# A fused attention and feed-forward kernel: beta turned early, longer fp32 dummies in the head, one tile written in halves, a zero fill moved behind a cast

## The chip, the cores and the metric

The kernel runs on one core of a Trainium2 chip. PE is TensorE (PEld its weight loads), DVE is VectorE, ACT is ScalarE, POOL is GpSimd. The metric is the device time in microseconds (us), the median over several executions. The profile times one execution's "span" on the core; it is about 1.8 us shorter than the device time. All timed executions below are in the fast state; one single run (e5) is of state unknown, as single runs on one core are. Ratios are the mean time of one kernel's fast runs over that of the other's fast runs of the same rounds, so they are not quite the ratio of the medians quoted.

## The reference

```python
# q, k, v: (8, 8, 576, 64) f32;  w_in: (512, 2048);  w_out: (2048, 512);  beta: (2048,)
q_s = softmax(q, over the 64 features);   k_s = softmax(k, over the 576 positions)
kv  = einsum('bhsd,bhse->bhde', k_s, v)
x   = einsum('bhsd,bhde->bhse', q_s, kv)  -> 4608 tokens x 512
h   = x @ w_in
out = (h * sigmoid(beta * h)) @ w_out     # float32
```

## The kernel before

The tokens are worked off in nine slabs of 512. A slab has "pass 1" (16 tiles f of 4 matmuls m with `WIN`, then a Silu on ACT) and "pass 2" (64 matmuls with `WOUT`). Everything before the first pass 1 is the head: it loads Q, K and V of batch 0 and the weights, takes exponentials (`EQ`, `EK`), transposes the queries on PE, forms the small KV matrices (`KVD`) and the tile `XT`.

`w_in` comes in five column chunks. They are loaded as fp32 and cast to bf16 by POOL (chunk 0, half of 1) and DVE (the rest). Chunk 1 serves tiles 2 and 3, chunk 2 tiles 4 to 7, chunk 3 tiles 8 to 11, chunk 4 tiles 12 to 15.

```python
WCH = ((0, 256), (256, 256), (512, 512), (1024, 512), (1536, 512))   # first column, width
...
def homes_ek(i, e_, r=()):                       # zeros in EK, on POOL
    z = EK[i][64 * e_:64 * e_ + 64, :, :, 64 * (1 - e_):64 * (2 - e_)]
    add(POOL, lambda e: e.memset(z.bitcast(F32), 0.0), r=r, w=[("ekz", i, e_)])
...
def warm(n, bk, long=False):                     # dummies that keep PE busy
    w = WARM[:, :].bitcast(F32) if long else WARM
    for _ in range(n):
        mm(PS[bk][:, 0:256] if long else PS[bk][:, :], w[:, 0:128], w[:, :], True, True, ...)
...                                              # the head, in program order
warm(6, 0, True)
exp_q(0); exp_kh(...)                            # ACT
norm_main(0, 0, 1); norm_main(0, 1, 1, POOL)     # softmax of the queries
go(t_steps(0, (0,), HEAD))                       # 4 transposes on PE
warm(3, 0, True)
norm_main(0, 2, 1, POOL); norm_main(0, 3, 1)
go(t_steps(0, (1,), HEAD))
warm(1, 0, True)
for m in (0, 2): load_win(0, m, 2)
for c in range(1, len(WCH)): load_win(c)
cast_v(...)
for m in range(NM): cast_win(0, m, 1, POOL)
cast_win(1, 0, 2, POOL)
for e_ in range(2):
    homes_ek(1, e_, [("win", 3, NM - 1)])        # nothing has written ("win", 3, 3) yet: no wait
go(t_steps(0, (2,), HEAD))
turn_beta()                                      # 6 tiny fp32 transposes
cast_v(0, 1, DVE)
go(t_steps(0, (3,), (1,)))
ksum(...); warm(2, 0)
...
out_now(0, 0, 4, ACTE)                           # XT of head pair 0, copied whole by ACT
...
cast_win(1, 2, 2, DVE)                           # second half of chunk 1
for m in range(1, NM): at(m)                     # tiles 0 and 1
for c in range(2, len(WCH)):
    for m in range(NM): cast_win(c, m, 1, DVE)
```

Dependencies are found in program order: an operation waits for the last writer of a key that stands before it. So the read of `("win", 3, 3)` in `homes_ek` did nothing. During pass 2 of slab 0, the attention of batch 1 is done at fixed steps (one step per matmul); `TT` and the `out_now(1, ...)` calls belong to that. I call it the crossing.

The softmax here doesn't subtract the row's maximum and nothing guards it: scores larger than these inputs give would overflow.

## Time and profile before

| | before |
|---|---|
| timed runs | 287.0 us median (286.8 to 287.31) |
| the execution that was profiled | 287.53 us, span 285.7, mean granted clock 0.992 |
| PE busy | 97% of the span |

The page's second part shows the span in 40 slices of 7.1 us, digits in tenths.

```profile
PE   7999999999999999999999999999999999999994
...
PEclk9899999999999999999999999999999999999999
DMA  7999999995899999207970033002800020021022
```

PE is full after the first slice, so only the head and the places where PE waits have time to give. The clock is below full in the second slice, and DMA is at 90% or more from the second to the ninth. The windows view of before shows the first of these closer. Its columns are the window, its length, busy us of PE, PEld, DVE, ACT and POOL with their instruction counts, the granted clock, the DMA share and GB/s.

```profile
10.00:12.00 2.00, 2.00 (x32) 1.58 (x32) 1.62 (x5) 1.98 (x2) 0.88 (x2) 0.88 1.01 377
12.00:14.00 2.00, 1.79 (x29) 1.56 (x28) 0.73 (x4) 0.50 (x2) 1.54 (x4) 0.50 1.03 349
14.00:16.00 2.00, 1.95 (x16) 0.94 (x15) 0.75 (x3) 1.17 (x2) 1.41 (x4) 0.76 1.07 381
```

The clock records of the trace put it exactly: 0.5 from 11.53 to 14.95 us. The first record is at 4.71 us, and the views print 1.00 before it; but the dummies there come 0.427 us apart, and 0.216 after it, so PE began at half clock. "Clock 1.00" below means from the first record on. The waits of PE (who waited for whom, us in total, times, longest):

```profile
PE PS L364 <- DVE WARM L221: 1.2, 1, 1.2
PE PS L362 <- DVE EQ L332: 0.6, 1, 0.6
PE PS L364 <- DVE WIN L585: 0.6, 1, 0.6
PE PS L364 <- DVE KVD L401: 0.5, 2, 0.3
PE PS L362 <- POOL EQ L332: 0.4, 2, 0.2
```

The timeline of DVE in before (start, us, operation, count, idle before it) shows the casts of chunk 1 (first line), 2, 3 and 4:

```profile
17.25 1.36 DVE L585 CAST WIN<-WST 128x512 bf16<-128x512 f32 x1
...
18.69 1.36 DVE L585 CAST WIN<-WST 128x512 bf16<-128x512 f32 x4
22.02 1.43 DVE L585 CAST WIN<-O2S 128x512 bf16<-128x512 f32 x4 [1.97 <-DMA O2S<-in_moe_w_in_dram]
24.73 1.44 DVE L585 CAST WIN<-O2S 128x512 bf16<-128x512 f32 x4 [1.27 <-DMA O2S<-in_moe_w_in_dram]
```

The timeline of POOL in before, the zero fill:

```profile
16.17 2.16 POOL L237 MEMSET EK<- 64x1152 f32 x2
```

And of PE in before: the wait for chunk 1, and the start of pass 2.

```profile
18.67 11.83 PE L364 MATMUL PS<-XT,WIN 128*128 128x512 bf16 x54 [0.55 <-DVE WIN L585]
30.34 1.03 PE L364 MATMUL PS<-WOUT,GT 128*128 128x512 bf16 x4
```

One cast of chunk 1 took 1.36 us where four casts of the same shape took 1.36 us together, and PE waited for it. At the crossing, PE's timeline of before has the wait for KVD and the first matmuls of slab 1:

```profile
45.17 0.39 PE L364 MATMUL PS<-QT,KVD 128*128 128x512 bf16 x1 [0.28 <-DVE KVD L401]
...
46.49 0.59 PE L364 MATMUL PS<-XT,WIN 128*128 128x512 bf16 x2
```

### The profile page before, as it was taken

How to read it: one execution, taken by the hardware profiler on the slowest of the kernel's cores; microseconds unless marked ns; L12 is line 12 of the kernel's file. 1: busy time of each engine (PE TensorE's matmuls, PEld its weight loads, DVE VectorE, ACT ScalarE, POOL GpSimd, SP SyncE). 2: the span in 40 equal slices, each digit the busy share in tenths (PEclk: the TensorE clock that was granted, in tenths of full speed). 3: DMA queues.
4: the chain of work that ended last, by engine and by line, in shares of the span. 5: the costliest groups of instructions: out<-in, count | busy, mean ns of one | idle time of the engine just before them, and what ended most of it. 6: DMA issues, size and time to landing. Idle time of an engine off the chain costs nothing.

```text
span 285.7 us, 3896 instructions
## 1 busy us (share of the span) xinstructions
PE 278.5 (97%) x1586; PEld 138.5 (48%) x1586; DVE 115.8 (41%) x212; ACT 177.4 (62%) x241; POOL 38.7 (14%) x60
## 2 busy tenths in 40 slices
PE   7999999999999999999999999999999999999994
PEld 5645445444455445544454445444544444444441
DVE  3765696109691248114741564055705200110021
ACT  5788486889977945796479737892650186028500
POOL 6640031305303032300140000000000000000000
PEclk9899999999999999999999999999999999999999
DMA  7999999995899999207970033002800020021022
GB/s 244 376 384 414 384 384 379 307 389 102 228 411 218 385 330 345 59 13 239 384 119 1 2 147 75 2 1 106 131 4 0 30 119 0 0 87 62 0 73 73
DMA packets 41438, 50.07 MB, mean 175 GB/s; under 512 B 20166, under 2 KB 29386, under 8 KB 40140
## 3 DMA queue, kind: packets, MB, share of 16 engines
q1 hardware_dynamic: 40556, 48.77, 53.6%
q10 hardware_dynamic: 864, 1.05, 1.1%
q8 instruction: 12, 0.20, 0.3%
q14 instruction: 6, 0.05, 0.1%
HBM read 36.71 MB, written 9.44 MB: 161 GB/s over the span
## 4 chain that ended last, share of the span: by engine, by line
PE 94%; DVE 2%; DMA 1%; POOL 1%; issue 0%; ACT 0%; POOLq 0%
PE PS L364 93%; DMA QF<-in_q_dram 1%; PE PS L362 1%; POOL EQ L332 1%; DVE QS L330 0%; DVE WIN L585 0%; DVE KVD L401 0%; DVE XT L534 0%; DVE EQ L332 0%; DVE O2S L726 0%; ACT EQ L293 0%; DVE QI L331 0%; DVE BC L605 0%; DVE RC L422 0%; DVE BETA L608 0%
## 5 line engine op out<-in xcount | busy, mean ns | idle before, releaser
L672 ACT ACTIVATE GT<-PS,BETA 128x512 bf16<-128x512 f32 x144 | 97.5, 688 | 77.9 <-PE PS L364 77.8
L364 PE MATMUL PS<-XT,WIN 128*128 128x512 bf16 x576 | 132.2, 379 | 0.6 <-DVE WIN L585 0.6
L364 PE MATMUL PS<-WOUT,GT 128*128 128x512 bf16 x576 | 132.7, 379 | 0.0
L364 PEld LDWEIGHTS PS<-XT,WIN 128*128 128x128 bf16 x576 | 60.1, 106 | 59.6 <-DVE WIN L585 1.0
L364 PEld LDWEIGHTS PS<-WOUT,GT 128*128 128x128 bf16 x576 | 54.6, 98 | 62.8 <-DVE O2S L726 0.2
L726 DVE COPY O2S<-PS 128x512 f32<-128x512 f32 x34 | 23.3, 686 | 110.7 <-PE PS L364 110.7
L364 PE MATMUL PS<-VB,EK 128*128 128x65 bf16 (+2 forms) x306 | 36.6, 197 | 0.0
L349 POOL CAST VB<-VF 128x576 bf16<-128x576 f32 (+1 forms) x31 | 22.7, 732 | 73.0 <-DMA VF<-in_v_dram 37.4
L305 ACT ACTIVATE EK<-KF 64x1152 bf16<-64x1152 f32 x24 | 27.8, 1158 | 0.4
L364 PEld LDWEIGHTS PS<-VB,EK 128*128 128x128 bf16 x306 | 23.0, 102 | 7.2 <-issue 0.5
L330 DVE TENSOR_REDUCE QS<-EQ 128x8 f32<-128x512 bf16 (+1 forms) x22 | 20.1, 914 | 3.6 <-ACT EQ L293 3.5
L439 DVE CAST XT<-PS 128x512 bf16<-128x512 f32 x24 | 16.4, 690 | 10.9 <-PE PS L364 10.9
L293 ACT ACTIVATE EQ<-QF 128x512 bf16<-128x512 f32 x32 | 17.9, 619 | 4.6 <-DMA QF<-in_q_dram 4.3
L332 DVE TENSOR_TENSOR EQ<-EQ,QI 128x1024 bf16<-128x1024 bf16 (+1 forms) x15 | 16.4, 1093 | 0.5
L364 PE MATMUL PS<-QT,KVD 128*128 128x512 bf16 (+1 forms) x36 | 12.4, 366 | 0.5 <-DVE KVD L401 0.5
L332 POOL TENSOR_TENSOR EQ<-EQ,QI 128x512 bf16<-128x512 bf16 x7 | 7.3, 1042 | 32.9 <-DVE QI L331 32.6
L315 ACT ACTIVATE EK<-KF 64x1152 bf16<-64x1152 f32 (+1 forms) x10 | 9.5, 966 | 1.6 <-DMA KF<-in_k_dram 1.5
L364 PE MATMUL PS<-WARM 128*128 128x256 f32 (+1 forms) x22 | 7.5, 490 | 1.2 <-DVE WARM L221 1.2
L401 DVE TENSOR_TENSOR KVD<-PS,RC 64x128 bf16<-64x128 f32 (+1 forms) x22 | 7.7, 349 | 1.6 <-PE PS L364 0.9
L338 DVE TENSOR_REDUCE QRS<-EQR 128x8 f32<-128x512 bf16 x4 | 2.7, 680 | 13.4 <-ACT EQR L320 13.4
L672 ACT ACT_TABLE_LOAD x5 | 6.4, 1283 | 0.1
L293 ACT ACT_TABLE_LOAD x5 | 6.4, 1283 | 0.1
(50 smaller groups left out, 77.9 us busy)
## 6 DMA issues: line engine op xcount, KB each, us to landing
out_dram<-O2S SPq DMA_DIRECT2D x8, 1024.0 KB, 5.2
KF<-in_k_dram SPq DMA_DIRECT2D x6, 1152.0 KB, 8.3
VF<-in_v_dram SPq DMA_DIRECT2D x6, 1152.0 KB, 11.9
QF<-in_q_dram SPq DMA_DIRECT2D x6, 1024.0 KB, 7.5
KF<-in_k_dram SPq DMA_DIRECT2D x8, 288.0 KB, 7.4
VF<-in_v_dram SPq DMA_DIRECT2D x8, 288.0 KB, 7.4
O2S<-in_moe_w_in_dram SPq DMA_DIRECT2D x2, 1024.0 KB, 13.6
WST<-in_moe_w_out_dram SPq DMA_DIRECT2D x2, 1024.0 KB, 9.2
```

Source lines behind the costliest of these rows:

```text
L293: add(ACTE, lambda e, o=o, a=a: e.activation(o, a, ACT.Exp), r=[("qf", i, hp)], w=[("eq", i, hp)])
L305: add(ACTE, lambda e, o=o, a=a: e.activation(o, a, ACT.Exp), r=[("kf", i, h) for h in hps], w=[("ek", i, h, e_) for h in hps])
L315: add(ACTE, lambda e: e.activation(o, a, ACT.Exp), r=[("kf", i, h) for h in hps], w=[("ek", i, h, e_) for h in hps])
L330: add(DVE, lambda e: e.tensor_reduce(s_, a, AX.X, ALU.add), r=ks, w=[("qs", i, hp0)])
L332: add(eng, lambda e: e.tensor_tensor(a, a, vb, ALU.mult), r=ks + [("qi", i, hp0)], w=ks)
L349: add(eng, lambda e: (e.copy if eng == ACTE else e.tensor_copy)(o, a), r=[("vf", i, hp), ("vone", i)], w=[("vb", i, hp, h) for h in ((0, 1 ...
L362: add(PE, lambda e: e.transpose(o, l, r_), r=r, w=w, bank=[bk])
L364: add(PE, lambda e: e.matmul(o, l, r_, start=start, stop=stop), r=r, w=w, bank=[bk])
L401: add(DVE, lambda e, o=o, a=a, s_=s_: e.tensor_tensor(o, a, s_, ALU.mult), r=[("ps", bk)] + [("rc", i, h) for h in hps], w=[("kvd", i, h, ...
L439: add(eng, lambda e: (e.copy if eng == ACTE else e.tensor_copy)(XT[i][:, hp, :], PS[bk][:, :]), r=[("ps", bk)], w=[("xt", i, hp)], bank=[bk])
L672: add(ACTE, lambda e: e.activation(GT[:, f, :], PS[bk][:, :], ACT.Silu, scale=BETA[:, f:f + 1]), r=[("ps", bk), "beta"], w=[("gt", f)], ba ...
L726: add(eng, lambda e: (e.copy if eng == ACTE else e.tensor_copy)(O2S[t % 2][:, u, :], PS[bk][:, :]), r=[("ps", bk)], w=[("o2", t % 2, u)], ...
```

## The change

The intent is to keep PE's clock up through the head and to let pass 1 start sooner. There are five parts: (1) the dummies become fp32 matmuls of 512 columns, placed between all the transposes; (2) beta is loaded right behind the first queries and turned after the first transposes, where PE would idle; (3) `XT` of pair 0 is copied in halves by DVE and ACT; (4) the zero fill of the second `EK` is moved behind the casts, so that its gate is real; (5) at the crossing, `out_now(1, 0)` and `out_now(1, 1)` come at the last step.

```diff
+        add(DVE, lambda e: e.memset(XT8[:, 0:2, :].bitcast(F32), 0.0), w=["xw"])
...
         def warm(n, bk, long=False):
-            w = WARM[:, :].bitcast(F32) if long else WARM
             for _ in range(n):
-                mm(PS[bk][:, 0:256] if long else PS[bk][:, :], w[:, 0:128], w[:, :], True, True,
-                   r=["warm"], w=[("ps", bk)], bk=bk)
+                if long:
+                    mm(PS[bk][:, :], bass.AP(XT8, 0, [[NM * SM, 128], [1, 256]]).bitcast(F32),
+                       bass.AP(XT8, 0, [[NM * SM, 128], [1, 1024]]).bitcast(F32), True, True,
+                       r=["xw"], w=[("ps", bk)], bk=bk)
+                else: ...                                      # as before
...
-        load_k(0, 4)
         for i, n in enumerate((2, 4)): ...                     # the load of beta
+        load_k(0, 4)
...
-        warm(6, 0, True)
+        warm(3, 0, True)
...
         go(t_steps(0, (0,), HEAD))
-        warm(3, 0, True)
+        turn_beta()
+        warm(1, 0, True)
...
-        for e_ in range(2):
-            homes_ek(1, e_, [("win", 3, NM - 1)])
         go(t_steps(0, (2,), HEAD))
-        turn_beta()
+        warm(1, 0, True)
...
-            if t < 2 and m > 1:
+            if (t, m) in ((0, 0), (0, 2), (0, 3), (1, 2), (1, 3)):
...
-        TT = (116, 126.5)
+        TT = (116, 128)
...
-        out_now(0, 0, 4, ACTE)
+        out_halves(0, 0, 4, 6)
...
         for c in range(2, len(WCH)):
             for m in range(NM):
                 cast_win(c, m, 1, DVE)
+        for e_ in range(2):
+            homes_ek(1, e_, [("win", 3, NM - 1)])
...
-                todo += [(126, lambda: out_now(1, 0, 7, DVE))]
+                todo += [(127.5, lambda: (out_now(1, 0, 7, DVE), out_now(1, 1, 1, ACTE)))]
...
-                out_now(1, 1, 1, ACTE)
```

Cut: the numbers of PSUM banks, and one key that guards XT8's later use.

More of the change, by code (lines that the diff above doesn't have):

```diff
@@ L471, in one @@
                     add(DVE, lambda e: e.tensor_copy(o, PS[bk][:, :]), r=[("ps", bk)],
-                        w=[("xt8", pi)], bank=[bk])
+                        w=[("xt8", pi), "xw"], bank=[bk])
             return [lambda hp=hp, e_=e_: one(hp, e_) for hp in range(NHP) for e_ in range(2)]
@@ L495, in warm @@
         def warm(n, bk, long=False):
-            w = WARM[:, :].bitcast(F32) if long else WARM
             for _ in range(n):
-                mm(PS[bk][:, 0:256] if long else PS[bk][:, :], w[:, 0:128], w[:, :], True, True,
-                   r=["warm"], w=[("ps", bk)], bk=bk)
+                if long:
+                    mm(PS[bk][:, :], bass.AP(XT8, 0, [[NM * SM, 128], [1, 256]]).bitcast(F32),
+                       bass.AP(XT8, 0, [[NM * SM, 128], [1, 1024]]).bitcast(F32), True, True,
+                       r=["xw"], w=[("ps", bk)], bk=bk)
+                else:
+                    mm(PS[bk][:, :], WARM[:, 0:128], WARM[:, :], True, True, r=["warm"],
+                       w=[("ps", bk)], bk=bk)
         def ksum(b, hp, kb):
@@ L701, in bass_efficient_attn_shen__then__act_swish_beta_kernel @@
         kv_mm(0, 2, 5, 0, D + 1)
-        out_now(0, 0, 4, ACTE)
+        out_halves(0, 0, 4, 6)
         kv_mm(0, 3, 5, 1, D + 1)
-        out_now(0, 1, 6, ACTE)
+        out_now(0, 1, 7, ACTE)
         ksum_inv(0, 5, 2, 2, D, VW)
@@ L707, in bass_efficient_attn_shen__then__act_swish_beta_kernel @@
         at(0)
-        out_halves(0, 2, 7, 3)
-        out_halves(0, 3, 4, 5)
+        out_halves(0, 2, 3, 4)
+        out_halves(0, 3, 6, 7)
         beta = read_beta()
```

## The prediction

> **What bounds it now.** Median 287.0 us, span 285.7. The page gives PE 97%, and the chain of waits is PE from 18.67 us to 281.9 but for about 1 us near 45 us. So only the head (0 to 27 us) and the crossing to the second slab (45 to 50 us) have time to give. The PE wait view lists 1.2 us (start), 0.6 and 0.4 (normalised queries), 0.6 (weight cast L585) and 0.5 (KVD, 0.3 of it at 45.17).
>
> In the head, by timeline and windows:
> - The granted clock is 0.50 from about 11.6 to 14.9 us, then 1.00[...]. In the 3.4 us before it PE streamed little: three sets of transposes, one short dummy, the beta turn (six tiny matmuls, 0.87 us), one-column ksum matmuls. The KV matmuls then cost about 60 ns each; the same at 43 us take about 30.
> - The cast of weight chunk 1 on DVE took 1.36 us (17.25 to 18.61), later ones of its shape 0.36 to 0.42: the second EK zero fill on POOL ran 17.25 to 18.33.[...] Pass 1 waited until 18.67.
> - DMA is full (0.9 to 1.1) from 2 us on. V lands in pieces until 12.5 us; weight chunk 2 about 18.2, 3 at 22.0, 4 at 24.7 (DVE waits).
>
> **What the change does.** The first dummies keep their work (3 of 512 columns for 6 of 256; start 0.25 us later, behind a larger memset). The beta turn moves to the gap after the first transposes, and three 0.85 us dummies fill 7.4 to 10.5 us. I expect clock 1.00 through 11.5 to 15. Estimate from these durations: first KVD 0.8 us earlier, XT 0 in halves another 0.2, the second KV and XT copies follow; without the zero fill chunk 1 is cast by about 16.5. Pass 1's third tile could start up to 2 us earlier.
>
> **How much counts.** Most is given back to the weight DMA, which nothing here speeds up. Chunk 2 (cast from 18.6) stops PE first. Chunk 3's last cast ends 23.45, where PE needed it at 24.07: at most 0.57 us remain. The zero fill, now really gated, runs 23.5 to 25.7 and holds chunk 4's casts (24.73) back to 25.7 to 27.1; PE needed the last at 27.53: 0.4 us remain. The later output steps hide the 0.28 us KVD wait at 45; I count 0.2. Sum: 0.6 us.
>
> **Predicted: 286.4 us, range 285.6 to 287.2; faster by over 2%: 0.01, within 2%: 0.98, slower: 0.01.**
>
> **Right if:** clock 1.00 in 11.5 to 15 us; chunk 1 cast in about 0.4 us before 17; new PE waits on casts of chunks 2, 3 or 4; chunk 3 landing near 22.0; the first chunk 4 cast stretched to over 1 us; pass 2 starting near 29.9 instead of 30.34; nothing above 0.1 us at 45.
>
> **Wrong if:** the clock still drops (now around 15 to 18): half-speed pass 1 costs up to 1 us and the time is 287 or more; the weight DMA lands earlier, or the zero fill misses chunk 4: 285.8 or better; the beta turn waits for beta behind the queries and delays the transposes.

Why the clock dropped is not shown by the trace: that a fuller PE would keep it at 1.00 was the author's estimate. That the fill held the cast was read from one overlap in it (fill to 18.33, cast to 18.61); e2 and e6 bear on the first, e3 on the second.

## The result, and the profile after

| | before | after |
|---|---|---|
| median (range), 4 runs each | 287.13 us (286.8 to 287.31) | 286.91 us (286.47 to 287.13) |
| ratio after/before, 95% interval | | 0.9992 (0.9974 to 1.0009) |
| the profiled execution | span 285.7, clock 0.992 | span 285.1, clock 1.000 |

The medians differ by 0.2 us, inside the noise. The two traces differ by 0.6 us, just what was predicted for the kernel. These two facts do not agree, and most of what follows is about that. First the trace of after, line for line against before. Its windows view:

```profile
10.00:12.00 2.00, 1.92 (x30) 1.31 (x30) 1.67 (x5) 1.98 (x3) 0.66 (x1) 1.00 1.02 391
12.00:14.00 2.00, 1.57 (x35) 1.30 (x35) 1.02 (x5) 0.93 (x2) 1.48 (x3) 1.00 1.07 369
14.00:16.00 2.00, 1.88 (x19) 0.84 (x15) 1.56 (x6) 1.30 (x4) 1.43 (x4) 1.00 1.07 374
```

The clock is full. The waits of PE in after:

```profile
PE PS L365 <- DVE XT L221: 1.5, 1, 1.5
PE PS L363 <- DVE EQ L333: 0.6, 1, 0.6
PE PS L365 <- DVE KVD L402: 0.4, 1, 0.4
PE PS L365 <- ACT EK L316: 0.2, 1, 0.2
```

The timeline of DVE in after, the same four chunks:

```profile
16.73 0.42 DVE L590 CAST WIN<-WST 128x512 bf16<-128x512 f32 x1
...
18.46 1.44 DVE L590 CAST WIN<-WST 128x512 bf16<-128x512 f32 x4 [1.15 <-DMA WST<-in_moe_w_in_dram]
21.16 1.43 DVE L590 CAST WIN<-O2S 128x512 bf16<-128x512 f32 x4 [1.27 <-DMA O2S<-in_moe_w_in_dram]
25.17 1.43 DVE L590 CAST WIN<-O2S 128x512 bf16<-128x512 f32 x4 [2.58 <-DMA O2S<-in_moe_w_in_dram]
```

The timeline of POOL in after:

```profile
22.72 2.17 POOL L238 MEMSET EK<- 64x1152 f32 x2 [6.33 <-DVE WIN L590]
```

Chunk 1 is cast 1.46 us sooner (it ends at 17.15 instead of 18.61). Then DVE waits for chunk 2 to land. The PE wait view does not show that PE waits too, because the modelled ends of the matmuls hide it. The weight loads on PE's timeline (PEld) in after do:

```profile
18.94 0.10 PEld L365 LDWEIGHTS PS<-XT,WIN 128*128 128x128 bf16 x1 [0.55 <-DVE WIN L590]
...
19.95 0.55 PEld L365 LDWEIGHTS PS<-XT,WIN 128*128 128x128 bf16 x4 [0.24 <-DVE WIN L590]
```

PE then starts pass 2 0.67 us sooner than in before's trace:

```profile
29.67 1.67 PE L365 MATMUL PS<-WOUT,GT 128*128 128x512 bf16 x7
```

And at the crossing in after:

```profile
44.53 0.39 PE L365 MATMUL PS<-QT,KVD 128*128 128x512 bf16 x1
...
45.79 0.59 PE L365 MATMUL PS<-XT,WIN 128*128 128x512 bf16 x2 [0.21 <-ACT EK L316]
```

The wait for KVD is gone, and a wait of 0.21 us has come a little later, where slab 1 starts. From the start of pass 2 to that matmul it took 46.49 - 30.34 = 16.15 us in before and 45.79 - 29.67 = 16.12 us in after. The part at the crossing gave 0.03 us.

### The profile page after: what moved, and what is told of

It is laid out like the page before. It is cut to its first block, busy times and chain, and to the rows that moved or that the text cites. A ratio compares the mean times of both kernels' runs of the same rounds, so it can differ in the third digit from the quotient of the medians.

```text
span 285.1 us, 3855 instructions
## 1 busy us (share of the span) xinstructions
PE 276.7 (97%) x1548; PEld 135.6 (48%) x1579; DVE 116.1 (41%) x214; ACT 177.1 (62%) x241; POOL 38.2 (13%) x60
## 4 chain that ended last, share of the span: by engine, by line
PE 82%; DMA 8%; SPq 5%; ACT 2%; issue 1%; DVE 1%; ACTq 0%
PE PS L365 82%; DMA O2S<-in_moe_w_in_dram 5%; DMA KF<-in_k_dram 3%; SPq L261 2%; ACT EK L316 2%; SPq L584 1%; SPq L251 1%; DVE WIN L590 0%; DVE O2S L732 0%; ACT GT L676 0%; SPq L550 0%; ACT O2S L732 0%; SPq L563 0%; ACTq L142 0%
## 5 line engine op out<-in xcount | busy, mean ns | idle before, releaser
L365 PE MATMUL PS<-WOUT,GT 128*128 128x512 bf16 x563 | 131.2, 379 | 0.6
L365 PE MATMUL PS<-VB,EK 128*128 128x65 bf16 (+2 forms) x306 | 35.7, 191 | 0.4
L350 POOL CAST VB<-VF 128x576 bf16<-128x576 f32 (+1 forms) x31 | 22.1, 714 | 73.2 <-DMA VF<-in_v_dram 53.7
L365 PEld LDWEIGHTS PS<-VB,EK 128*128 128x128 bf16 x306 | 22.1, 98 | 7.0 <-issue 0.3
L365 PE MATMUL PS<-QT,KVD 128*128 128x512 bf16 (+1 forms) x36 | 11.6, 351 | 0.5 <-DVE KVD L402 0.4
L365 PE MATMUL PS<-XT 128*128 128x512 f32 x12 | 7.9, 786 | 1.5 <-DVE XT L221 1.5
L339 DVE TENSOR_REDUCE QRS<-EQR 128x8 f32<-128x512 bf16 x4 | 2.7, 680 | 13.4 <-ACT EQR L321 13.4
```

The costliest lines, as they stand in the source:

```text
L350: add(eng, lambda e: (e.copy if eng == ACTE else e.tensor_copy)(o, a), r=[("vf", i, hp), ("vone", i)], w=[("vb", i, hp, h) for h in ((0, 1 ...
L365: add(PE, lambda e: e.matmul(o, l, r_, start=start, stop=stop), r=r, w=w, bank=[bk])
```

## The experiments

Twelve runs. The theories, as the expectations name them:
- **A**: the gain is real and comes from freeing the cast of chunk 1; the landing of chunk 2 cuts it down.
- **B**: the gain of the one pair of traces is an accident of the clock in the one traced run of before. **D** is B made exact: that execution was unlucky, and others of before are as fast as the change.
- **C**: the half clock in the head is what costs.
- **E**: what a faster head wins is lost again at 68 us.
- **F**: pass 2 starts at the latest of several sums.

### e1 to e4: the whole change again, and parts of it

These four ran on one chip with nine runs of before (median 286.81, 286.48 to 287.06).

e1_whole is the change itself. 

> The whole change again, for a tighter interval. Theory A (the gain is the freed cast of weight chunk 1, cut down by the landing of weight chunk 2): 0.4 to 0.7 us faster than before (ratio 0.9976 to 0.9986), granted clock 1.00 from 11.5 to 15 us, pass 1 held for a few tenths of a us by the casts of chunk 2 near 18.9 us, pass 2 starting 0.6 to 0.7 us earlier than in the profile of before (30.34). Rival B (the gain of the one trace is the state of the clock in that one run of before): ratio 0.999 to 1.000.

e2_dummies is before with parts 1 and 2 only. Edit: the dummy, beta and K load hunks of the diff above. 

> Before plus only the long dummies, the early beta load and the early beta turn. Theory A: clock 1.00 from 11.5 to 15 us, KV matmuls at about 30 ns instead of 60, but the cast of chunk 1 still waits for the EK zero fill on POOL (to about 18.3 us), so under 0.2 us gained (ratio 0.9993 to 1.0005). Rival C (the half-speed clock in the head is what costs): at least 0.5 us gained, as much as the whole change (ratio 0.998 or less).

e3_fill is before with part 4 only:

```diff
-        for e_ in range(2):
-            homes_ek(1, e_, [("win", 3, NM - 1)])
         go(t_steps(0, (2,), HEAD))
...
         for c in range(2, len(WCH)): ...  cast_win(c, m, 1, DVE)
+        for e_ in range(2):
+            homes_ek(1, e_, [("win", 3, NM - 1)])
```

> Before plus only the late, really gated zero fill. Theory A: the clock still drops for about 3.4 us, but the cast of chunk 1 takes about 0.4 us instead of 1.36 and the 0.55 us PE wait at 18.67 is gone: 0.4 to 0.6 us gained (ratio 0.9979 to 0.9988). Rival C: no gain (ratio 0.9995 or more).

e4_nodummies is parts 3, 4 and 5 without 1 and 2. 

> The whole change without the dummies and the beta moves (zero fill late, XT of pair 0 in halves, crossing steps later). Theory A: the PE arrives at chunk 2 later than in the whole change but still about when its casts end, so within 0.2 us of the whole change. Rival C: at least 0.5 us slower than the whole change, near before.

| run | median (range) | ratio to before (95%) | pass 2 starts | span of that trace |
|---|---|---|---|---|
| e1_whole | 286.90 (286.69 to 287.40) | 1.0008 (0.9995 to 1.0020) | 29.60 | 284.9 |
| e2_dummies | 286.75 (286.69 to 286.95) | 1.0000 (0.9988 to 1.0013) | 29.16 | 285.0 |
| e3_fill | 286.69 (286.63 to 287.21) | 1.0002 (0.9990 to 1.0015) | 29.23 | 284.9 |
| e4_nodummies | 286.92 (286.72 to 287.27) | 1.0006 (0.9992 to 1.0019) | 29.31 | 285.1 |

No part gains anything that intervals of about 0.35 us to either side would show, nor does the whole. A and C both fall as statements on the time. Two things are odd, and they carry the explanation. First, e3_fill and e4_nodummies have the old short dummies and still had no drop in the head (clock 1.00 from 6.99 and 5.19 us on). Second, e2_dummies starts pass 2 earlier than the whole change, although it keeps the early zero fill, and yet it ends no sooner. Its PE waits have a line that neither before nor after has:

```profile
PE PS L365 <- DMA QTR<-EQR: 0.4, 1, 0.4
```

`QTR` are the remainder queries, transposed by DMA and used at 68 us in slab 1. In e1, e2, e3 and e4 PE starts slab 1's pass 2 at 60.67, 60.36, 60.36 and 60.38 us, but the first `QTR` matmul at 67.94, 68.02, 67.95 and 68.14: the three that came 0.3 us earlier started it no earlier. From that matmul to the end it took 216.95 to 217.06 us in every trace that has these steps where before has them (before, after, e1 to e6, e9, e11), so a lead is kept or lost by 68 us. The weight load of that matmul waits for the transpose in before and after too (0.47 and 0.45 us on PEld), though PE's own view shows no gap there.

### e5: another trace of before

> The kernel before, unchanged, for a second trace of it. Theory D (the first trace of before was an unlucky execution[...]): clock 1.00 from 7 us on, span 284.7 to 285.3 instead of 285.7, pass 2 starting at 29.2 to 29.7 us instead of 30.34, i.e. the head of the kernel before is as fast as that of the whole change. Rival A (before is always held by the half clock and the zero fill): pass 2 again near 30.3, span near 285.7.

It took 287.53 us, span 285.7, beside eleven timed runs of before on that chip with median 286.70 (286.53 to 287.64). The clock was 1.00 from 5.22 us on, so D was right about the clock and wrong about the span: this execution was slow as well, for another reason. Without the drop, chunk 1 no longer set the time, although the early fill still stretched its cast to 1.21 us. Its DVE timeline:

```profile
16.56 1.21 DVE L585 CAST WIN<-WST 128x512 bf16<-128x512 f32 x1
...
18.44 1.61 DVE L585 CAST WIN<-WST 128x512 bf16<-128x512 f32 x4 [0.52 <-DMA WST<-in_moe_w_in_dram]
22.64 1.43 DVE L585 CAST WIN<-O2S 128x512 bf16<-128x512 f32 x4 [2.59 <-DMA O2S<-in_moe_w_in_dram]
25.35 1.43 DVE L585 CAST WIN<-O2S 128x512 bf16<-128x512 f32 x4 [1.28 <-DMA O2S<-in_moe_w_in_dram]
```

Its PE timeline:

```profile
17.83 12.75 PE L364 MATMUL PS<-XT,WIN 128*128 128x512 bf16 x54 [0.40 <-DVE WIN L585]
30.41 0.81 PE L364 MATMUL PS<-WOUT,GT 128*128 128x512 bf16 x3
```

PE passed chunk 1 at 17.83 us, 0.84 us sooner than in the first trace of before, and still started pass 2 at 30.41. The 54 matmuls took 12.75 us instead of 11.83, because chunk 3 landed at 22.64.

**Theory F.** Tiles 4 and on can't start before their chunk is cast. A steady matmul takes (30.34 - 18.67) / 54 = 0.216 us. Behind the last cast of chunk 1, 2, 3 and 4 there are still 54, 45, 29 and 13 matmuls to run before pass 2. With 0.06 us from cast to PE, pass 2 starts at the latest of: end of chunk 1's cast + 11.7, of chunk 2's + 9.8, of chunk 3's + 6.3, of chunk 4's + 2.9, and PE's own pace: once tiles 0 and 1 have had their first matmul, 62 remain, so the start of that run + 13.4. The table takes the ends of the casts from the DVE timelines of all runs but e8, later ones too (us; the latest sum in bold). The 0.216 us come from the first row, which therefore fits by construction; the other rows are a test.

| trace | chunk 1 | chunk 2 | chunk 3 | chunk 4 | latest sum | pass 2 measured | span |
|---|---|---|---|---|---|---|---|
| before, first | **18.61** | 20.05 | 23.45 | 26.17 | 30.33 | 30.34 | 285.7 |
| e5, before again | 17.77 | 20.05 | **24.07** | 26.78 | 30.39 | 30.41 | 285.7 |
| e6_cold | **18.36** | 19.80 | 22.06 | 25.79 | 30.08 | 30.09 | 285.4 |
| after, first | 17.15 | **19.90** | 22.59 | 26.60 | 29.68 | 29.67 | 285.1 |
| e1_whole | 16.90 | **19.82** | 22.51 | 26.12 | 29.60 | 29.60 | 284.9 |
| e2_dummies | 17.10 | **19.37** | 21.91 | 26.09 | 29.15 | 29.16 | 285.0 |
| e3_fill | 16.92 | **19.45** | 22.18 | 26.16 | 29.23 | 29.23 | 284.9 |
| e4_nodummies | 16.68 | **19.52** | 22.23 | 25.79 | 29.30 | 29.31 | 285.1 |
| e7_fill_outr | 16.84 | 19.52 | 23.37 | **26.94** | 29.81 | 29.83 | 285.3 |
| e11_before_split | 17.49 | **19.77** | 22.60 | 25.31 | 29.55 | 29.55 | 285.4 |
| e9_split | 17.16 | 19.13 | 22.10 | 25.50 | PE, 29.09 | 29.10 | 284.9 |
| e10_best | 16.93 | 18.75 | 21.47 | 25.25 | PE, 28.86 | 28.87 | 284.3 |
| e12_best_nodummies | 16.83 | 18.68 | **22.57** | 25.27 | 28.89 | 28.91 | 284.4 |

The sums fit every trace within 0.03 us. The landings behind them differ: DVE's first cast of chunk 3 began between 20.48 (e2) and 22.64 us (e5) in the kernels with whole loads. These kernels differ in the head, and the traces come from several chips. But two traces of one kernel, before and e5, lie 0.62 us apart, and e3 and e7, whose programs are the same up to slab 1, lie 1.20 us apart (20.74 and 21.94). So the scatter is as large as what the change does. The change takes away the first sum only, and the second lies at 29.2 to 29.8 with whole loads.

### e6: what a dropped clock costs

```diff
-        warm(3, 0, True)          # behind the first transposes
-        warm(1, 0, True)          # behind the second
-        warm(2, 0)                # behind ksum
```

> Before without the dummies between and behind the transposes (the six at the start stay)[...]. Theory D: clock 0.50 for about 3.4 us somewhere in 8 to 18 us, and the time 0.3 to 0.9 us above before (ratio 1.001 to 1.003): this is what the dummies of before already buy, so the longer ones of the change can buy nothing more. Rival C (a dropped clock in the head is given back to the DMA waits): within 0.1 us of before.

Windows view of e6_cold:

```profile
8.00:10.00 2.00, 0.91 (x8) 0.65 (x8) 1.90 (x5) 1.98 (x4) 1.57 (x2) 0.65 1.05 402
10.00:12.00 2.00, 2.00 (x32) 1.79 (x31) 1.83 (x5) 1.81 (x2) 1.19 (x2) 0.50 1.04 369
12.00:14.00 2.00, 1.79 (x33) 1.60 (x30) 0.86 (x4) 0.46 (x1) 1.39 (x5) 0.50 1.08 354
```

The clock was 0.5 from 8.61 to 15.44 us, 6.83 us and not the 3.41 of before; the mean granted clock was 0.987 or 0.988 in five of the six executions, and 0.993 in the sixth. The median was 287.21 us, ratio 1.0011 (0.9998 to 1.0025): about 0.3 us, the low end of what D expected, with an interval that just reaches zero. So C's rival form (all of it given back) is not excluded, but even 6.8 us at half clock cost no more than about 0.7 us.

How often does it drop? 3.4 us at half clock take 0.006 off the mean over the span, so I read a mean below 0.995 as a drop. (The clock also halves near the end of the span, from 284.60 us in before, 285.06 in after and 282.62 in e10; that gives means such as e10's 0.997.) With the short dummies in place (before, e3, e4, e5, e7, e11, e12) I count it in 6 of 59 recorded executions, the first trace of before, which raised the question, left out; with the long ones (after, e1, e2, e8, e9, e10) in 0 of 31. That points to the long dummies doing what they were meant to do, but with so few it is not shown. Nor is it shown what makes the clock drop: in before, from the transposes at 8.34 us to the drop at 11.53, the longest idle on PE's timeline was 0.24 us, while it ran transposes, dummies, tiny and one-column matmuls; e11 has the same PE work there, and its traced execution kept its clock (mean 0.999). In e11 the two executions with a dropped clock took 287.52 and 287.77 us, and the other four 286.60 to 287.23. But a drop is not always paid for: e4's one such execution took 286.72, the fastest of its five. With at most 0.7 us in one execution of ten, the mean gain would be at most about 0.07 us (my estimate from these counts).

### e7 and e8: the wait at 68 us, and halved weight loads, with a mistake

```diff
-                todo = spread(outr_steps(1), 97, 101) + attn_late(2)
+                todo = spread(outr_steps(1), 123, 127) + attn_late(2)
```

e7_fill_outr is e3_fill with this edit. 

> The late zero fill (as in e3_fill) and the remainder queries' output steps of the second slab moved from steps 97 to 101 to steps 123 to 127, so that PE no longer waits at 68 us for their transpose by DMA. Theory E (a faster head is given back at 68 us, where that transpose lands at the same time whatever PE does): 0.2 to 0.5 us faster than before (ratio 0.9983 to 0.9993), no PE wait at 68 us. Rival (the gain is lost somewhere else, or there is none): ratio 0.9995 or more.

e8_split_outr is the whole change with this edit and with the loads of chunks 2 to 4 halved:

```diff
         for c in range(1, len(WCH)):
-            load_win(c)
+            nm = 2 if c in (2, 3, 4) else NM
+            for m in range(0, NM, nm):
+                load_win(c, m, nm)
```

(the keys of the staging buffers are split to match). 

> The whole change, the same move of the remainder's output steps, and weight chunks 2 to 4 loaded in two halves each, so that the first half can be cast before the whole has landed. If the landing of chunk 2 is what holds the whole change back: no PE wait on the chunk 2 casts near 18.9 us, pass 2 starting 0.3 to 0.8 us before 29.6, and 0.4 to 1.0 us faster than before (ratio 0.9965 to 0.9986). If not: pass 2 near 29.6 again and a gain of 0.2 us or less.

Both gave wrong results (relative error 0.17): by step 123 the KV steps of batch 2 have written over the `KVD` that the remainder's output of batch 0 still reads. There is no race, only the wrong order. e7 was no faster (median 287.13, ratio 1.0008, 0.9990 to 1.0026). Its trace is not slow at 68 us, but at chunk 4, in the way the prediction feared for the change. POOL in e7_fill_outr:

```profile
23.49 2.17 POOL L237 MEMSET EK<- 64x1152 f32 x2 [7.48 <-DVE WIN L585]
```

DVE in e7_fill_outr:

```profile
24.64 2.30 DVE L585 CAST WIN<-O2S 128x512 bf16<-128x512 f32 x4 [1.27 <-DMA O2S<-in_moe_w_in_dram]
```

Chunk 3 landed late here (21.94), so the gated fill ran until 25.66 and the four casts of chunk 4 took 2.30 us instead of 1.43. e7 does not settle E. e8 (median 286.37, ratio 0.9985, 0.9971 to 0.9999) started pass 2 at 28.80, but I draw nothing on the time from a wrong kernel; e9 does it properly.

### e9 to e12: does the change pay once the weights no longer hold PE?

These ran on one chip with eleven runs of before (median 287.11, 286.57 to 287.61).

e9_split is the whole change with the halved loads. 

> The whole change with weight chunks 2 to 4 loaded in two halves each, and nothing else moved (correct, unlike e8_split_outr). Theory F (the start of pass 2 is the latest of several sums: cast of chunk 1 + 11.7 us, first cast of chunk 2 + 11.2, of chunk 3 + 7.8, last cast of chunk 4 + about 2.9; the change removes the first only): pass 2 starts at 28.5 to 29.2 us, the remainder's transpose takes back a part at 68 us, and the time is 0.2 to 0.6 us below before (ratio 0.9979 to 0.9993). Rival: no gain, ratio 0.9996 or more.

e10_best adds two edits, with the order of `KVD` kept (the step numbers are written short):

```diff
-            homes_ek(1, e_, [("win", 3, NM - 1)])
+            homes_ek(1, e_, [("win", 4, NM - 1)])
...                                                # the remainder's output, slab 1
-        spread(outr_steps(1), 97, 101)
+        spread(outr_steps(1), 100.5, 104.2)
...                                                # KV and output steps behind it
-        99, 103 / 105, 109 / 110, 123
+        101, 105 / 106, 110 / 111, 124
```

> As e9_split, the zero fill gated by the last cast of chunk 4 instead of chunk 3, and the remainder's output steps and the KV steps behind them 2 to 3.5 steps later (still before KVD is written over). Theory F with give-back at 68 us: no cast of chunk 4 above 0.5 us, and 0.4 to 1.0 us below before (ratio 0.9965 to 0.9986), at least as fast as e9_split. Rival (nothing is given back at 68 us): equal to e9_split within 0.1 us.

e11_before_split is before with the halved loads only. 

> The kernel before with only the halved loads of weight chunks 2 to 4. Theory F: the zero fill still delays the cast of chunk 1 to 17.1 to 18.6 us, so pass 2 starts at 28.8 to 30.3 us, later than in e9_split, and the gain is 0.3 us at most (ratio 0.999 to 1.000). If the halved loads alone are what counts: as fast as e9_split.

e12_best_nodummies is e10_best without parts 1 and 2 of the change. 

> e10_best without the long dummies and the beta moves (short dummies as before). If the clock in the head is worth something once the weights are no longer the limit: executions with a dropped clock (mean granted clock 0.994 or less) are slower by 0.3 us or more, and the mean is 0.1 to 0.5 us above e10_best. If the dummies buy nothing even then: within 0.1 us of e10_best.

| run | median (range) | ratio to before (95%) | pass 2 starts | first QTR matmul |
|---|---|---|---|---|
| e9_split | 286.62 (286.28 to 287.16) | 0.9985 (0.9970 to 1.0000) | 29.10 | 67.97 |
| e10_best | 286.36 (286.07 to 286.50) | 0.9974 (0.9961 to 0.9988) | 28.87 | 68.07 |
| e11_before_split | 287.20 (286.60 to 287.77) | 1.0004 (0.9988 to 1.0019) | 29.55 | 68.44 |
| e12_best_nodummies | 285.91 (285.76 to 286.20) | 0.9962 (0.9948 to 0.9975) | 28.91 | 68.28 |

Halved loads without the change gain nothing, and with it about 0.4 us, with an interval that just reaches 1. DVE in e9_split casts chunks 1 and 2 without the fill, and half of chunk 2 early:

```profile
16.74 0.42 DVE L590 CAST WIN<-WST 128x512 bf16<-128x512 f32 x1
...
17.24 0.69 DVE L590 CAST WIN<-WST 128x512 bf16<-128x512 f32 x2
18.37 0.76 DVE L590 CAST WIN<-WST 128x512 bf16<-128x512 f32 x2 [0.44 <-DMA WST<-in_moe_w_in_dram]
```

PE in e9_split then runs through to pass 2 without a wait:

```profile
15.70 13.56 PE L365 MATMUL PS<-XT,WIN 128*128 128x512 bf16 x62
29.10 2.11 PE L365 MATMUL PS<-WOUT,GT 128*128 128x512 bf16 x9
```

e11 differs. POOL in e11_before_split:

```profile
16.16 2.33 POOL L237 MEMSET EK<- 64x1152 f32 x2
```

DVE in e11_before_split:

```profile
16.33 1.16 DVE L585 CAST WIN<-WST 128x512 bf16<-128x512 f32 x1
...
17.57 2.20 DVE L585 CAST WIN<-WST 128x512 bf16<-128x512 f32 x4
```

The early zero fill now also hits the casts of chunk 2, which have become ready sooner (2.20 us for four instead of about 1.44). The same cast of chunk 1 took 0.62 (e2), 1.06 (e6), 1.16 (e11), 1.21 (e5) and 1.36 us (before) with the early fill, and 0.42 us in e3 with the late one; in before and e6 it ended 0.28 us after the second memset of the fill (18.61 after 18.33, 18.36 after 18.08). So in before two causes stood one behind the other: the fill, and the landing of whole chunks. With either alone taken away a cast still holds PE (e3, e11); with both away PE's own pace is the limit (e9, e10). What that is worth in time is less clear. Pass 2 starts only 0.13 us sooner in e9's trace than in e3's (29.10 and 29.23), and both have a span of 284.9, so e9's gain lies in its timed runs alone, at the edge of the noise. Clear of it are e10 and e12, which also move the steps at 68 us; no run moved those steps alone.

E is supported but not settled. e9 (pass 2 started 1.24 us sooner than in before's trace, the first `QTR` matmul 0.81 us) lost part of its lead at 68 us, as its PE timeline shows:

```profile
67.97 0.20 PE L365 MATMUL PS<-QTR,KVD 128*128 128x64 bf16 x1 [0.51 <-DMA QTR<-EQR]
```

In e10_best no such wait is listed, and from the start of pass 2 to the end it took 284.3 - 28.87 = 255.4 us, against 255.8 in e9. The ratios, 0.9985 and 0.9974, point the same way with intervals that overlap.

e12 is the fastest kernel, 1.2 us below before by the medians and clear of noise. It is correct, and it has the short dummies. The long dummies and the beta moves gained nothing on top: e12's five times (285.76 to 286.20) lie almost wholly below e10's five (286.07 to 286.50), though the intervals overlap. Neither expectation was met: e12 was to be 0.1 to 0.5 us slower than e10, or within 0.1 us of it. No clock drop fell into those five, so what the long dummies save when it does drop was not tested here. Why the kernel with them should be slower, by some 0.3 us, stays open: the two traces (284.4 and 284.3) do not show it, for the traced execution was the slowest of e12's five and the fastest of e10's.

## Why the prediction was right or wrong

The number, 286.4 us with 285.6 to 287.2, held: 286.91 in the first runs, 286.90 in the next. That says little, for the range also holds the 287.0 of before itself. The gain of 0.6 us did not hold: the measured ratios, 0.9992 and 1.0008, show none.

- **"What bounds it now", the failing step.** The prediction read one trace and took it for the kernel. That execution took 287.53 us where the median was 287.0, with a mean clock of 0.992. The half clock and the fill together made chunk 1 the latest sum there, at 30.33. In most executions of before the clock doesn't drop (2 of 31 timed ones beside the experiments). In e5, the same kernel without the drop, chunk 1's sum is 29.5, below chunk 2's 29.8 and chunk 3's 30.4; in e2, which also keeps the early fill but not the drop, it is 28.8, below chunk 2's. So the 0.6 us were won against a slow execution: 7 of the 31 timed ones of before are as long (span 285.6 or more), 2 of them with a drop. No trace of a fast execution of before was caught: both traces have span 285.7, and most timed ones have 284.7 to 285.2. That such executions are held by chunk 2, as e2 and e3 are, follows from the sums but was not seen, so this step is argued and not shown.
- **Clock 1.00 from 11.5 to 15 us:** right in after, but e3 and e4 have it too with the short dummies.
- **Chunk 1 cast in about 0.4 us before 17:** right (0.42 us, 16.73).
- **"Chunk 2 stops PE first":** right, and it is the whole bound in the change: 0.55 us of weight-load wait at 18.94, pass 2 at 29.67 (29.9 was expected).
- **Chunk 3 lands near 22.0; 0.57 us remain:** wrong as a fixed time. It was cast from 21.16 in after, and over the runs from 20.48 to 22.64.
- **The fill holds back chunk 4; 0.4 us remain:** it happened in e7 (2.30 us instead of 1.43, pass 2 set by it), but in after the fill ended at 24.89, before chunk 4 came at 25.17. It happens where chunk 4 lands before the fill, gated by chunk 3's last cast, has ended: a little in e4 (1.68 us), also in e9 (2.80 us). The prediction said that the time would be 285.8 or better if the weights landed earlier or the fill missed chunk 4. Both happened in after, and the time was 286.91: that branch failed too, for chunk 2 held PE first.
- **0.2 us at the crossing; nothing above 0.1 us at 45:** mis-sized. It gave 0.03 us between the two traces; the wait for KVD became one of 0.21 us at the first matmul of slab 1.
- **Not foreseen:** the DMA transpose at 68 us, which takes back what a faster head wins (about 0.3 to 0.5 us of PE wait in e2, e3, e4 and e9).

## What to carry to other kernels

Before explaining half a microsecond from a trace, compare the traced execution's own time and clock with the median of the timed runs; if it is slower than all of them, its critical path may not be the kernel's. Where several loads gate one stream of matmuls, write the start of the next stage as the latest of "release + matmuls still to run", for each load: it tells which parts must be removed together. Here no single part gained anything measurable; the fill and the whole loads removed together did so at the edge of the noise (e9), and clearly with the steps at 68 us moved as well (e10, e12). And fixed step numbers for a late consumer should be checked against what overwrites its operands; a check for races does not find a wrong order.
